# Three layers, one core: the put-aside tiles of the second layer are loaded three f ahead, and the sums of W_in's quarters are stored once and loaded afterwards

## The chip, the core and the metric

One NeuronCore of a Trainium2 chip runs the whole program. Its engines are TensorE (PE, with weight loads as PEld), VectorE (DVE), ScalarE (ACT), GpSimd (POOL) and SyncE (SP), which issues nearly all DMAs. The metric is the device time of one execution in microseconds; lower is better.

## What is computed

```python
x = _attn(q, k, v, phi)             # 8 batches x 576 tokens, read as 4608 x 512
g, val = xn @ w_gate, xn @ w_val    # first layer, xn = rms-normed x, d_ff 1536
x = (silu(g) * val) @ w_out
h = x @ w_in                        # second layer, 512 -> 2048
r = np.maximum(h, 0.0)
return ((r * r) @ w_out).astype(np.float32)
```

All is float32. Each operand of a matmul is split into a high and a low part (`split`, L64: ScalarE makes the high part, VectorE the low one), and three matmuls make one product. This case is about the second layer.

## The kernel before

The 4608 tokens are 9 blocks of 512 (`T`). `phase_b` (L999) takes them in four wide pairs (p = 0 to 3, two blocks each) and a last pair of half the width (p = 4, one block in two halves). In the profile the five pairs start at about 871, 1049, 1233, 1417 and 1598 us.

The first product, x @ W_in, is done for a pair by a Strassen-like scheme of seven products. W_in's 16 tiles of 128 columns (f) are taken two at a time: eight quarters q = 0 to 7, with f0 = 2q and f1 = 2q + 1. A quarter's weights are four pieces A11, A12, A21, A22 and four sums S1 to S4 of them. The order of the products in a quarter is b1 (A11), b2 (A12), b6 (S2), b7 (S3), b5 (S1), b3 (S4), b4 (A22); they rotate through four PSUM banks. VectorE adds them up to c11, c21, c22, c12, applies relu and square, and the results of the first block of the pair go on as `gh`/`gl`.

While quarter q is multiplied, the weights of q + 1 are made ready: `wi2_sums` (L909, four GpSimd operations write `si_s`), `wi2_split` "a" (A11, A12: `wiha`, `wila`), "b" (the four sums, 128 x 1024: `wihb`, `wilb`), "c" (A22: `wihc`, `wilc`). At the end of the quarter `wi2_load` (L902) loads the raw weights of q + 2 in two DMAs of 256 KB (`si`), the second of which waits until `wilc` has been made from its buffer. All this is done anew in each of the five pairs.

The second product, with W_out, goes in pieces between the products: `z` for the first block of the pair, f by f. What belongs to the second block is put aside in DRAM: c12 and c22 are stored as `gd[f]` (256 KB each). After the eight quarters the kernel finishes `z`, stores the block (`out_store`, four tiles of 256 KB; each store writes its 128 rows as chunks of 32 rows, so its pattern in DRAM begins with a dimension of 4, or is two stores with a dimension of 2 where a batch ends), and then runs the loop over f = 0 to 16 (L1114) for the second block, `zz`: load `gd[f]` into `gb` (two buffers, one load ahead), split it, and multiply f - 1, 12 matmuls. In the same loop `x2_step` makes the next pair's x operands, from `xr`, which `x2_load` loads in two halves: the first at the end of quarter 6, the second at f = 6 of the loop. The output stores of the second block come in quarters 0 and 1 of the next pair.

Each engine takes its instructions in the order of the program, and SP too: a DMA that has to wait holds up those behind it.

Of the kernel before, what the change touches and what calls it, by code (L numbers as in the profile page):

```python
# [9 lines left out]
F32 = mybir.dt.float32  # L10
# [10 lines left out]
P = 128  # L21
# [31 lines left out]
class Kernel:  # L53
# [67 lines left out]
    def run(self):  # L121
        nc, tc, ctx = self.nc, self.tc, self.ctx
        self.raws, self.started, self.wo_next, self.st = {}, [], [], {}
        const = ctx.enter_context(self.pool("const"))
        dram = ctx.enter_context(self.pool("dram", space=DRAM))
        ps = ctx.enter_context(self.pool("ps", space=PSUM))
        self.ps, self.dram = ps, dram

        self.ident = const.tile([P, P], F32, name="ident")
        make_identity(nc, self.ident)  # L130
        self.ones = const.tile([P, P], F32, name="ones")
        nc.vector.memset(self.ones, 1.0)
        self.g_sb = const.tile([P, KC], F32, name="g_sb")
        self.idle = self.ones.bitcast(BF16)

        self.y1 = [dram.tile([P, KC, HALF], F32, name=f"y1_{n}") for n in range(2 * B)]
        self.w1d = [dram.tile([P, KC * DM], F32, name=f"w1_{n}") for n in range(NCH)]
        self.w2d = {(c, f): dram.tile([P, DM], F32, name=f"w2_{c}{f}") for f in range(NF2) for c in "iz"}

        wa, up = self.pool("wa"), self.pool("up")  # L140
        self.wa, self.up = wa.__enter__(), up.__enter__()
        cms = []
        with tc.using_default_side("right"):
            for name in ("raw", "wst", "at"):
                cms.append(self.pool(name))
                setattr(self, name, cms[-1].__enter__())

        with tc.manual_schedule():
            self.make_plan()
            self.prologue()  # L150
            self.phase_a(0, NI * (B - 1) + 3)


        for cm in reversed(cms):
            cm.__exit__(None, None, None)
        with tc.using_default_side("right"):
            self.wb = ctx.enter_context(tc.tile_pool(name="wb1", bufs=1, reuse_waits="tile"))
        self.w2, self.w2_raw, self.w2_loaded, self.wi, self.x2 = {}, {}, 0, {}, {}
        with tc.manual_schedule():
            self.phase_a(NI * (B - 1) + 3, NI * B + 1)  # L160
        up.__exit__(None, None, None)
        wa.__exit__(None, None, None)
        self.wb2 = ctx.enter_context(tc.tile_pool(name="wb2", bufs=1, reuse_waits="tile"))
        with tc.manual_schedule():
            self.phase_b()
# [663 lines left out]
    def phase_a(self, start, end):  # L829
        nc = self.nc  # L830
        if not start:
            self.us = {}
        for n in range(start, end):
            first = True
            if n < len(self.items):
                b, hf, f, first, _ = self.items[n]
                gp = self.ps.tile([P, T], F32, tag="g", name=f"g{n}")[:, 0:HALF]
                self.mm_in(gp, b, hf, f, 0)
                self.slot(n, "a")
                sl = self.up.tile([P, HALF], F32, tag="sl", bufs=2, name=f"sl{n}")  # L840
                nc.scalar.activation(sl, gp, AF.Silu)  # L841
                vp = self.ps.tile([P, T], F32, tag="v", name=f"v{n}")[:, 0:HALF]
                self.mm_in(vp, b, hf, f, 1)
                self.slot(n, "b")
                nc.vector.tensor_tensor(sl, sl, vp, op=ALU.mult)  # L845
                uh = self.up.tile([P, HALF], F32R, tag="uh", bufs=3, name=f"uh{n}")
                ul = self.up.tile([P, HALF], F32R, tag="ul", bufs=3, name=f"ul{n}")
                self.split(uh, ul, sl, lo_engine="pool")
                self.us[n] = (uh, ul)
                self.slot(n, "c")  # L850

            second = 0 < n and n - 1 < len(self.items) and self.items[n - 1][3]
            for m in () if second else (n - 2, n - 1) if first else (n - 2,):
                if m >= 0:
                    self.mm_out(m)
            self.slot(n, "d")
            if NF1 <= n < NI and n % 6 == 3:
                t = self.up.tile([P, KC, HALF], F32, tag="st", name=f"yl{n}")
                nc.sync.dma_start(t, self.y1[2 * b + hf])
                self.st["y"] = t  # L860
            i = n - NI * (B - 1)
            if i == 4:
                self.x2_load(0, 0)
                self.wi2_load(0)
            elif i == 13:
                self.x2_load(0, 1)
            if 6 <= i < 13:
                self.x2_step(0, 0, i - 6)
            elif 15 <= i < 22:
                self.x2_step(0, 1, i - 15)  # L870
            elif i == 5:
                self.wi2_sums(0)
            elif i in (13, 14, 22):
                self.wi2_split(0, "abc"[(13, 14, 22).index(i)])
            elif i == 23:
                self.wi2_load(1)
                self.wo2_next(0)


# [19 lines left out]
        self.split(hi, lo, self.w2_raw.pop(i))  # L899
        self.w2[i] = (hi, lo)  # L900

    def wi2_load(self, q):  # L902
        self.wi_raw = []
        for i in range(2):
            t = self.wb.tile([P, DM], F32, tag=f"si{i}", name=f"si{q}_{i}")
            self.nc.sync.dma_start(t, self.w2d["i", 2 * q + i])
            self.wi_raw.append(t)

    def wi2_sums(self, q):  # L909
        eng = self.nc.gpsimd  # L910
        s0, s1 = self.wi_raw
        s = self.wb.tile([P, 4, 2 * P], F32, tag="ss", name=f"si{q}_s")
        a11, a12, a21, a22 = s0[:, 0 : 2 * P], s0[:, 2 * P : DM], s1[:, 0 : 2 * P], s1[:, 2 * P : DM]
        eng.tensor_tensor(s[:, 0], a21, a22, op=ALU.add)  # L914
        eng.tensor_tensor(s[:, 1], s[:, 0], a11, op=ALU.subtract)
        eng.tensor_tensor(s[:, 2], a11, a21, op=ALU.subtract)
        eng.tensor_tensor(s[:, 3], a12, s[:, 1], op=ALU.subtract)
        self.wi_sum = s

    def wi2_split(self, q, part):  # L920
        pool = self.wb2 if q % 2 else self.wb
        src = {
            "a": self.wi_raw[0],
            "c": self.wi_raw[1][:, 2 * P : DM],
            "b": self.wi_sum.rearrange("p s n -> p (s n)"),
        }[part]
        n = src.shape[-1]
        hi = pool.tile([P, n], F32R, tag=f"wih{part}", name=f"wih{part}{q}")
        lo = pool.tile([P, n], F32R, tag=f"wil{part}", name=f"wil{part}{q}")
        self.split(hi, lo, src)  # L930
        for i, k in enumerate({"a": ("A11", "A12"), "c": ("A22",), "b": ("S1", "S2", "S3", "S4")}[part]):
            self.wi[k, q % 2] = tuple(t[:, 2 * P * i : 2 * P * (i + 1)] for t in (hi, lo))

    def width(self, p):
        return T if p < NB // 2 else T // 2
# [63 lines left out]
    def phase_b(self):  # L999
# [22 lines left out]
        def z_pieces(n, y, key, f):  # L1022
# [6 lines left out]

            return [partial(do, 0), partial(do, 2)]  # L1030

        for _ in range(2):
            self.wo2_next(NF2)
        for p in range(NPAIR):
# [3 lines left out]
            for q in range(NQ):  # L1038
                if q == 1:
                    y = [self.ps.tile([P, T], F32, tag=f"y{c}", name=f"z{p}_{c}") for c in range(KC)]  # L1040
                nq = (q + 1) % NQ if p < NPAIR - 1 or q < NQ - 1 else None
                if q:
                    for f in (2 * q - 2, 2 * q - 1):
                        self.pieces += z_pieces(2 * p, y, (p, f), f)
                f0, f1 = 2 * q, 2 * q + 1
                more = nq is not None
                b1 = product("A11", "X11")
                p1 = work("cp", 3, f"p1_{p}_{q}", w)
                nc.scalar.activation(p1, b1, AF.Copy)
# [1 line left out]
                c11 = work("c", 4, f"c11_{p}_{q}", w)  # L1051
                nc.vector.tensor_tensor(c11, b2, p1, op=ALU.add)
                if more:
                    self.wi2_sums(nq)
                piece()
                b6 = product("S2", "T2")
                u = work("cp", 3, f"u_{p}_{q}", w)
# [4 lines left out]
                c21 = work("c", 4, f"c21_{p}_{q}", w)  # L1062
                nc.vector.tensor_tensor(c21, b7, u, op=ALU.add)
                if more:
                    self.wi2_split(nq, "a")
                piece()
                b5 = product("S1", "T1")
                nc.vector.tensor_tensor(u, b5, u, op=ALU.add)
# [5 lines left out]
                else:  # L1074
                    self.g_split(p, f1, 1, c22)
                if more:
                    self.wi2_split(nq, "b")
                piece()
                b3 = product("S4", "X22")
                c12 = work("c", 4, f"c12_{p}_{q}", w)  # L1080
# [8 lines left out]
                sq(c21)  # L1089
                self.g_split(p, f1, 0, c21)  # L1090
                if more:
                    self.wi2_split(nq, "c")
                    if p < NPAIR - 1 or q < NQ - 2:
                        self.wi2_load((q + 2) % NQ)
                piece()
                for _ in range(2):
                    self.wo2_next(NF2)
                if q == NQ - 2 and p + 1 < NPAIR:
                    self.x2_load(p + 1, 0)
            f0, f1 = NF2 - 2, NF2 - 1  # L1100
            for c in range(KC):
                self.mm_z(y, self.gs[p, f0], f0, c)
# [7 lines left out]
                self.out_store(2 * p, y, c, c + 1)  # L1110

            y = [self.ps.tile([P, T], F32, tag=f"y{c}", name=f"zz{p}_{c}") for c in range(KC)]
            loaded = {}
            for f in range(NF2 + 1):  # L1114
                while len(loaded) < min(f + 2, NF2):
                    i = len(loaded)
                    loaded[i] = work("gb", 2, f"gb{p}_{i}", w)
                    nc.sync.dma_start(loaded[i], gd[i])
                if f < NF2:
                    self.gs.pop((p, f), None)  # L1120
                    key = ("b", p, f)
# [79 lines left out]
```

## Time and profile before

| | |
|---|---|
| Times | 1716.00, 1712.21, 1714.54 us; median 1714.54 |
| The profiled execution | 1711.83 us, its span 1709.9 us |
| TensorE busy | 1565.5 us, 92% of the span |
| VectorE, ScalarE, GpSimd busy | 1061.7, 623.6, 508.7 us |
| Mean granted TensorE clock | 0.955 |
| DMA | 227.98 MB, 133 GB/s over the span |

All times within the span are from its start. The share of busy time is an average over stages; the second layer takes the time from about 840 us on. A matmul's duration in the trace overlaps the next one's: the pace is the difference of two starts. The granted clock is given as a share of the full 2.4 GHz, so 0.50 is 1.2 GHz. "DMA share" is the mean busy share of the 16 DMA engines.

### The profile page before, as it was taken

What the parts mean: (1) busy time and instruction counts of PE and PEld (TensorE: products, weight loads), DVE (VectorE), ACT (ScalarE), POOL (GpSimd) and SP (SyncE); (2) the same over time, 40 slices, a digit from 0 to 9 for tenths busy, and PEclk for the clock granted to TensorE, in tenths of its full rate; (3) what the DMA queues carried; (4) which work ended last, traced back from release to release, by engine and by line L of the source; (5) the groups of instructions that cost most, each with busy time, mean ns of one, the idle gap of its engine ahead of it and who ended that gap; (6) DMA issues with size and microseconds to landing.
All of it is one profiled execution on the core that took longest, in us unless ns stands there. A gap on an engine that the chain in (4) does not pass through costs nothing.

```text
span 1709.9 us, 26676 instructions
## 1 busy us (share of the span) xinstructions
PE 1565.5 (92%) x10302; PEld 1319.1 (77%) x10302; DVE 1061.7 (62%) x1744; ACT 623.6 (36%) x1240; POOL 508.7 (30%) x547
## 2 busy tenths in 40 slices
PE   5487999999999999999999969996999889996987
PEld 4266798888889798889988857885788668885876
DVE  4887756657574755535568845674577546773575
ACT  1566535354444435343433323222322232222232
POOL 1476544344443534234222200221012200220021
PEclk7688999999999999999999989998999989998999
DMA  9797573755546562322123333223322332223211
GB/s 258 226 278 278 214 219 135 219 184 168 176 170 185 193 194 110 113 93 97 46 88 110 118 102 89 87 70 121 99 85 70 116 112 81 74 74 117 73 46 43
DMA packets 129455, 227.98 MB, mean 133 GB/s; under 512 B 27440, under 2 KB 69424, under 8 KB 123184
## 3 DMA queue, kind: packets, MB, share of 16 engines
q1 hardware_dynamic: 125744, 223.39, 41.3%
q10 hardware_dynamic: 3584, 2.88, 0.7%
q8 instruction: 81, 1.33, 0.3%
q14 instruction: 46, 0.38, 0.1%
HBM read 174.72 MB, written 51.51 MB: 132 GB/s over the span
## 4 chain that ended last, share of the span: by engine, by line
PE 74%; DVE 8%; DMA 8%; ACT 4%; POOL 3%; issue 2%; SPq 2%; ACTq 0%; DVEq 0%; POOLq 0%
PE y L811 5%; PE y L812 5%; PE y L813 5%; PE h_S L985 4%; PE z L1141 3%; PE z L1143 3%; PE h_S L987 3%; PE z L1142 3%; PE h_S L986 3%; PE zz L1141 3%; DMA gb<-gd 3%; PE zz L1142 3%; PE zz L1143 3%; PE v L795 3%; PE g L795 3%; PE h_A L985 3%
## 5 line engine op out<-in xcount | busy, mean ns | idle before, releaser
L71 POOL TENSOR_TENSOR ul<-sl,uh 128x288 fp32r<-128x288 f32 x192 | 166.5, 867 | 363.7 <-ACT uh L67 363.3
L811 PE MATMUL y<-uh,woh 128*128 128x288 f32 x768 | 235.4, 307 | 0.0
L914 POOL TENSOR_TENSOR si_s<-si 128x256 f32<-128x256 f32 x40 | 33.5, 837 | 677.8 <-DMA si<-w_i 563.2
L812 PE MATMUL y<-uh,wol 128*128 128x288 f32 x768 | 227.7, 297 | 0.8 <-POOL wol L71 0.8
L813 PE MATMUL y<-ul,woh 128*128 128x288 f32 x768 | 226.5, 295 | 0.0
L845 DVE TENSOR_TENSOR sl<-sl,v 128x288 f32<-128x288 f32 x192 | 86.0, 448 | 178.6 <-PE v L797 140.0
L67 ACT ACTIVATE gh<-c 128x512 fp32r<-128x512 f32 (+1 forms) x96 | 53.8, 561 | 350.4 <-DVE c L1020 341.9
L1141 PE MATMUL zz<-bzh,gbh 128*128 128x512 f32 x256 | 104.6, 409 | 60.0 <-ACT gbh L67 60.0
L811 PEld LDWEIGHTS y<-uh,woh 128*128 128x128 f32 x768 | 144.7, 188 | 16.4 <-issue 15.5
L67 ACT ACTIVATE uh<-sl 128x288 fp32r<-128x288 f32 x192 | 85.2, 444 | 182.9 <-DVE sl L845 182.9
L812 PEld LDWEIGHTS y<-uh,wol 128*128 128x128 f32 x768 | 145.2, 189 | 1.7 <-POOL wol L71 1.0
L813 PEld LDWEIGHTS y<-ul,woh 128*128 128x128 f32 x768 | 145.0, 189 | 0.0
L841 ACT ACTIVATE sl<-g 128x288 f32<-128x288 f32 x192 | 78.4, 408 | 165.2 <-PE g L797 159.6
L795 PE MATMUL g<-anh,wph 128*128 128x288 f32 x384 | 119.9, 312 | 14.9 <-ACT sl L841 10.1
L1141 PE MATMUL z<-bzh,gh 128*128 128x512 f32 x320 | 127.0, 397 | 0.1
L1143 PE MATMUL z<-bzh,gl 128*128 128x512 f32 x320 | 126.0, 394 | 0.0
L1142 PE MATMUL z<-bzl,gh 128*128 128x512 f32 x320 | 125.6, 392 | 0.0
L795 PE MATMUL v<-anh,wph 128*128 128x288 f32 x384 | 120.4, 313 | 5.1 <-DVE sl L845 5.1
L796 PE MATMUL g<-anl,wph 128*128 128x288 f32 x384 | 115.4, 301 | 0.0
L796 PE MATMUL v<-anl,wph 128*128 128x288 f32 x384 | 115.3, 300 | 0.0
L797 PE MATMUL v<-anh,wpl 128*128 128x288 f32 x384 | 114.9, 299 | 0.0
L797 PE MATMUL g<-anh,wpl 128*128 128x288 f32 x384 | 114.2, 297 | 0.0
(214 smaller groups left out, 3966.8 us busy)
## 6 DMA issues: line engine op xcount, KB each, us to landing
w<-w SPq DMA_DIRECT2D x48, 1024.0 KB
si<-w_i SPq DMA_DIRECT2D x80, 256.0 KB
q<-in_q_dram SPq DMA_DIRECT2D x128, 144.0 KB
gd<-c SPq DMA_DIRECT2D x64, 256.0 KB
gb<-gd SPq DMA_DIRECT2D x64, 256.0 KB
y<-ys SPq DMA_DIRECT2D x16, 576.0 KB
raw_i<-in_moe_w_in_dram SPq DMA_DIRECT2D x16, 512.0 KB
raw_z<-in_moe_w_out_dram SPq DMA_DIRECT2D x16, 512.0 KB
```

The costliest lines, as they stand in the source:

```text
L67: nc.scalar.activation(hi, src, AF.Copy)
L71: eng.tensor_tensor(lo, src, hi.bitcast(F32), op=ALU.subtract)
L795: nc.tensor.matmul(out, wh[:, r, cs], ah[:, r], start=(r == 0), stop=False)
L796: nc.tensor.matmul(out, wh[:, r, cs], al[:, r], start=False, stop=False)
L797: nc.tensor.matmul(out, wl[:, r, cs], ah[:, r], start=False, stop=(r == NR - 1))
L811: nc.tensor.matmul(y, hi[:, cs], uh, start=first, stop=False)
L812: nc.tensor.matmul(y, lo[:, cs], uh, start=False, stop=False)
L813: nc.tensor.matmul(y, hi[:, cs], ul, start=False, stop=last)
L985: nc.tensor.matmul(out, wh[:, cs], xh, start=(kk == 0), stop=False)
L1141: nc.tensor.matmul(y[c], gh[:, cs], oh, start=(f == 0), stop=False)
L1142: nc.tensor.matmul(y[c], gh[:, cs], ol, start=False, stop=False)
L1143: nc.tensor.matmul(y[c], gl[:, cs], oh, start=False, stop=(f == NF2 - 1))
```

## The change

- `gb` has four buffers instead of two. At the end of quarter 6, behind `x2_load`, the first three `gd` tiles are loaded (`gb_load(3)`); in the loop over f, tile f + 3 is loaded at step f.
- The sums are made in the first pair only. There, `wi2_split` "b" also stores the split sums `wihb`, `wilb` into 16 DRAM tiles `sd` (512 KB each, two per quarter). From the second pair on, `wi2_sums` and `wi2_split` "b" do nothing, and `wi2_load` first loads the two `sd` tiles of the quarter into the same buffers, then `si` as before. The pair's number p is handed through.

```diff
+        self.sd = [[dram.tile([P, 4 * 2 * P], F32, name=f"sd{q}{i}") for i in "hl"] for q in range(NF2 // 2)]
...
-    def wi2_load(self, q):
+    def wi2_load(self, p, q):
         self.wi_raw = []
+        if p:
+
+            t = self.wi2_tiles(q, "b", 4 * 2 * P)
+            for x, d in zip(t, self.sd[q]):
+                self.nc.sync.dma_start(x.bitcast(F32), d)
+            self.wi2_set(q, "b", t)
         for i in range(2):
             t = self.wb.tile([P, DM], F32, tag=f"si{i}", name=f"si{q}_{i}")
             self.nc.sync.dma_start(t, self.w2d["i", 2 * q + i])
             self.wi_raw.append(t)
 
-    def wi2_sums(self, q):
+    def wi2_sums(self, p, q):
+        if p:
+            return
...
+    def wi2_split(self, p, q, part):
+        if p and part == "b":
+            return
...
+        t = self.wi2_tiles(q, part, src.shape[-1])
+        self.split(*t, src)
+        self.wi2_set(q, part, t)
+        if part == "b":
+            for x, d in zip(t, self.sd[q]):
+                self.nc.sync.dma_start(d, x.bitcast(F32))
...
+        def gb_load(end):
+            while len(loaded) < min(end, NF2):
+                i = len(loaded)
+                loaded[i] = work("gb", 4, f"gb{p}_{i}", w)
+                nc.sync.dma_start(loaded[i], gd[i])
...
                 if more:
-                    self.wi2_split(nq, "c")
+                    self.wi2_split(np, nq, "c")
                     if p < NPAIR - 1 or q < NQ - 2:
-                        self.wi2_load((q + 2) % NQ)
+                        self.wi2_load(p + (q + 2) // NQ, (q + 2) % NQ)
                 piece()
                 for _ in range(2):
                     self.wo2_next(NF2)
-                if q == NQ - 2 and p + 1 < NPAIR:
+                if q == NQ - 2 and wide:
                     self.x2_load(p + 1, 0)
+                    loaded = {}
+                    gb_load(3)
...
-            loaded = {}
             for f in range(NF2 + 1):
-                while len(loaded) < min(f + 2, NF2):
-                    i = len(loaded)
-                    loaded[i] = work("gb", 2, f"gb{p}_{i}", w)
-                    nc.sync.dma_start(loaded[i], gd[i])
+                gb_load(f + 4)
```

## Rows read from the trace of the kernel before

**Rows 1.** The page: engine, busy us (share of span) x instructions.

```profile
PE 1565.5 (92%) x10302; PEld 1319.1 (77%) x10302; DVE 1061.7 (62%) x1744; ACT 623.6 (36%) x1240; POOL 508.7 (30%) x547
```

**Rows 2.** Busy time by stretch: engines (x instructions), then clock, DMA share, GB/s.

```profile
1115.00:1145.00 30.00, 30.00 (x132) 24.50 (x131) 22.75 (x33) 7.28 (x12) 7.32 (x8) 1.00 0.22 71
1674.00:1682.00 8.00, 5.79 (x26) 4.71 (x25) 6.19 (x14) 2.55 (x7) 0.02 (x1) 0.79 0.21 66
```

**Rows 3.** Waits, us in total, times, longest: whole span; then 1595 to 1710 us.

```profile
PE zz L1141 <- ACT gbh L67: 60.0, 7, 14.3
...
PE h_S L985 <- DVE c L1081: 4.9, 4, 2.3
PE h_S L985 <- DVE c L1088: 2.4, 5, 0.7
```

**Rows 4.** Timeline of TensorE: start, us, operation [idle before <- releaser].

```profile
992.30 0.39 PE L1143 MATMUL z<-bzh,gl 128*128 128x512 f32 x1
1006.90 0.79 PE L1141 MATMUL zz<-bzh,gbh 128*128 128x512 f32 x1 [14.21 <-ACT gbh L67]
...
1012.12 0.40 PE L1141 MATMUL zz<-bzh,gbh 128*128 128x512 f32 x1
...
1558.42 0.80 PE L1141 MATMUL zz<-bzh,gbh 128*128 128x512 f32 x1 [14.21 <-ACT gbh L67]
```

**Rows 5.** Timeline of SP's queue around the first wide pair's end.

```profile
974.78 3.80 SPq L947 DMA_DIRECT2D xr<-y  x6
...
987.26 3.03 SPq L906 DMA_DIRECT2D si<-w_i  x2
991.31 3.23 SPq L1170 DMA_DIRECT2D out_dram<-os  x4
994.64 24.66 SPq L1118 DMA_DIRECT2D gb<-gd  x8
```

**Rows 6.** The chain that ended last, 950 to 1250 us: start, us, what.

```profile
994.64 11.50 DMA gb<-gd
```

**Rows 7.** Busy time by stretch, columns as in rows 2, during the stall.

```profile
994.00:996.00 2.00, 0.00 (x0) 0.00 (x0) 0.00 (x0) 0.00 (x0) 1.59 (x3) 0.74 0.22 70
...
998.00:1000.00 2.00, 0.00 (x0) 0.00 (x0) 0.00 (x0) 0.00 (x0) 0.00 (x0) 0.50 0.79 296
...
1002.00:1004.00 2.00, 0.00 (x0) 0.00 (x0) 0.00 (x0) 0.00 (x0) 0.00 (x0) 0.50 0.26 102
```

**Rows 8.** Busy time by stretch: weight loads of the first layer; x loads.

```profile
302.00:303.00 1.00, 1.00 (x10) 1.00 (x9) 1.00 (x4) 0.68 (x2) 0.15 (x1) 1.00 1.01 426
...
1026.00:1032.00 6.00, 5.34 (x24) 4.10 (x22) 0.69 (x1) 0.75 (x2) 0.00 (x0) 1.00 0.83 238
```

**Rows 9.** Timelines of ScalarE, VectorE, TensorE: quarter 1 of pairs two and three.

```profile
1076.55 0.63 ACT L67 ACTIVATE wiha<-si 128x512 fp32r<-128x512 f32 x1 [4.34 <-DMA si<-w_i]
1078.54 0.69 DVE L1070 TENSOR_TENSOR c<-h_S,u 128x512 f32<-128x512 f32 x1
1079.68 0.39 PE L985 MATMUL h_A<-X11h,wiha 128*128 128x512 f32 x1
...
1259.36 0.63 ACT L67 ACTIVATE wiha<-si 128x512 fp32r<-128x512 f32 x1 [2.94 <-DMA si<-w_i]
1263.89 0.39 PE L985 MATMUL h_A<-X11h,wiha 128*128 128x512 f32 x1
```

**Rows 10.** The chain that ended last, in the last pair.

```profile
1641.49 2.76 DMA si<-w_i
...
1647.83 1.07 ACT wihb L67
...
1648.92 1.23 DVE wilb L71
1650.15 0.34 DVE c L1081
...
1662.24 0.34 DVE c L1081
```

More of the change, by code (lines that the diff above doesn't have):

```diff
@@ L863, in phase_a @@
                 self.x2_load(0, 0)
-                self.wi2_load(0)
+                self.wi2_load(0, 0)
             elif i == 13:
@@ L871, in phase_a @@
             elif i == 5:
-                self.wi2_sums(0)
+                self.wi2_sums(0, 0)
             elif i in (13, 14, 22):
-                self.wi2_split(0, "abc"[(13, 14, 22).index(i)])
+                self.wi2_split(0, 0, "abc"[(13, 14, 22).index(i)])
             elif i == 23:
-                self.wi2_load(1)
+                self.wi2_load(0, 1)
                 self.wo2_next(0)
@@ L918, in wi2_sums, with wi2_tiles, wi2_set @@
         self.wi_sum = s
-    def wi2_split(self, q, part):
+    def wi2_tiles(self, q, part, n):
         pool = self.wb2 if q % 2 else self.wb
+        return [pool.tile([P, n], F32R, tag=f"wi{i}{part}", name=f"wi{i}{part}{q}") for i in "hl"]
+    def wi2_set(self, q, part, t):
+        for i, k in enumerate({"a": ("A11", "A12"), "c": ("A22",), "b": ("S1", "S2", "S3", "S4")}[part]):
+            self.wi[k, q % 2] = tuple(x[:, 2 * P * i : 2 * P * (i + 1)] for x in t)
+    def wi2_split(self, p, q, part):
+        if p and part == "b":
+            return
         src = {
@@ L926, in wi2_split @@
         }[part]
[L927 to L932, printed above, removed]
+        t = self.wi2_tiles(q, part, src.shape[-1])
[4 more added lines that the diff above has]
+                self.nc.sync.dma_start(d, x.bitcast(F32))
     def width(self, p):
@@ L1040, in phase_b @@
                     y = [self.ps.tile([P, T], F32, tag=f"y{c}", name=f"z{p}_{c}") for c in range(KC)]
-                nq = (q + 1) % NQ if p < NPAIR - 1 or q < NQ - 1 else None
+                np, nq = p + (q + 1) // NQ, (q + 1) % NQ
                 if q:
@@ L1045, in phase_b @@
                 f0, f1 = 2 * q, 2 * q + 1
-                more = nq is not None
+                more = np < NPAIR
                 b1 = product("A11", "X11")
@@ L1053, in phase_b @@
                 if more:
-                    self.wi2_sums(nq)
+                    self.wi2_sums(np, nq)
                 piece()
@@ L1064, in phase_b @@
                 if more:
-                    self.wi2_split(nq, "a")
+                    self.wi2_split(np, nq, "a")
                 piece()
@@ L1076, in phase_b @@
                 if more:
-                    self.wi2_split(nq, "b")
+                    self.wi2_split(np, nq, "b")
                 piece()
```

## The prediction

> **What bounds the kernel now.** I read the page's busy times first, then the table of waits, then the timelines of single engines where a wait ends last. TensorE is busy for 92% of the span [rows 1], and in the second layer's main loop it is busy for all of a 30 us stretch at the full granted clock [rows 2]. A cheaper VectorE, ScalarE or GpSimd step there gains nothing; only stretches where TensorE stands still count. The table of waits names them [rows 3]: 60.0 us in 7 waits for the split of a put-aside tile (`gb`), and 4.9 and 2.4 us in the half-width last pair.
>
> The 60 us are four long stalls at the start of the second block of each wide pair and three short ones in its middle. The first long one lasts 14.21 us, and the fourth is the same [rows 4]. What ends it is a chain of four 256 KB output stores issued from 991.31 on, then the first `gb` load, issued at 994.64 [rows 5], 11.50 us until that load lands at 1006.14 [rows 6], and 0.76 us for the split until TensorE starts at 1006.90. While it is awaited the DMA engines are busy for 0.26 of their time at 102 GB/s; only between 998 and 1000 did they reach 0.79 [rows 7]. I read this so: the stores use a quarter of the engines, about 25 GB/s each, and the `gb` load, spread over all 16, is done on the other twelve at once but waits on these four behind 1 MB of stores: 1 MB at 102 GB/s is 10.3 us. The Trainium skill, DMA: Bandwidth & Descriptors, section Why a DMA increments its semaphore by 16 and not by 1, says that a transfer runs on the largest number of engines up to 16 that divides the slowest dimension of both its patterns; the store's pattern in DRAM begins with a dimension of 4. Its section Queues, rings and completion order adds that each engine consumes its ring in order. The trace agrees with both (0.26 and 102 GB/s). By the second, the fourth tile can't pass the stores, and the loads ahead give the 28.0 us worked out below; without it they would give the 61.5 us of rival 1.
>
> **The loads ahead.** Now three tiles are loaded in the loop's seventh quarter, long before the stores. The fourth is still issued behind the last out_store, as the first is today; a fourth buffer doesn't change its place in the queue. So f = 0 to 2 can run during the drain, and f = 3 waits where f = 0 waits now.
>
> Worked out: f = 0 is split after the last ScalarE copy and starts some 1 us after 992.7. Three f at full clock take 3 x 2.73 = 8.2 us (12 matmuls each, at 30.00 us for 132 of them [rows 2]), until about 1002. The fourth tile lands at 1006.1 plus a delay d, and f = 3 starts at 1006.9 + d. Today f = 0 starts there. The gain is three f, 8.2 us, less d.
>
> d comes from the 1 MB of sums that the change puts on the queue just ahead of the stores, at about 987, before the `si` pair [rows 5]. Spread over 16 engines it is 64 KB on each. Nearest prices: 1 MB weight loads in the first layer move at 426 GB/s (2.4 us), the x and `gb` loads of the second layer at 238 GB/s (4.2 us) [rows 8]. The sums have 4 KB rows, nearer the former. As the engines are partly idle around 988 to 992, not all of it is seen: d is 0 to 2.8 us, and I take 1.2. Gain 7.0 us per pair (5.4 to 8.2), 4 pairs: **28.0 us**.
>
> The clock: after 14 us of idling the granted clock is 0.50, and f = 0 takes 5.22 us (1006.90 to 1012.12) instead of 2.73 [rows 4, 7]. It fell some 2.3 us after the engine stopped (the mean of 0.74 over 994 to 996). The remaining idle is about 6 us, so I expect the same fall and no gain; if the clock stayed up, 2.4 us more per pair, 9.6 in all.
>
> The three short stalls, 60.0 - 4 x 14.2 = 3.1 us, come because a `gb` load is queued behind the next pair's x loads. With three tiles ahead it has 8 us more, so they go, with about 0.3 us each of slowed first matmuls: **4.0 us**. What would be late next is ScalarE, which waits there for the x load before its next split; its slack is about 2 us.
>
> **The sums.** From the second pair on, each quarter drops four GpSimd operations, a 128 x 1024 ScalarE copy (1.07 us) and a VectorE subtraction (1.23) [rows 10], and adds two 512 KB loads on SP's queue, which wait for the matmuls of the same quarter, but the store queued before them waits for these anyway. In wide pairs this is beside a full TensorE: zero. In the first pair each quarter adds two stores, 1 MB. SP waits for the split's two halves, and the next store behind waits for later VectorE work anyway; 71 GB/s are in use in the main loop [rows 2], and 1 MB per 15 us adds 68. Nobody awaits their landing, so I take zero; work added gains nothing, and at worst one `si` load comes late behind them, once, by the 4.2 us that 1 MB takes at the slower pace of [rows 8].
>
> In the last pair the sums are on the path. The chain goes through the `si` load (2.76 us), GpSimd's four operations (1644.25 to 1647.83, 3.6 us), the copy, the subtraction and then the rest of the quarter, and comes round after 12.1 us (1650.15 to 1662.24 [rows 10]). TensorE alone needs less: 24 matmuls at 0.227 us and 42 of half the columns at half of that, an estimate from [rows 2], are 10.2 us. Without the sums the `si` load needs only to land before the next `a` split, and TensorE sets the pace. The waits for L1081 and L1088 are 7.3 us together [rows 3]. The first, 2.26 us, stays: there `si` lands late behind the stores, and the 1 MB ahead of it costs as much as the missing sums give back. So 5.1 us go, and with them the slow clock around 1678 (0.79 over 8 us, 1.7 us [rows 2]), of which I count 1.5: **6.6 us** (0 to 9).
>
> **A new wait.** In the second quarter of a pair the `si` load is already late, behind output stores: ScalarE waits for it until 1076.55 in the second pair, the sum c22 starts at 1078.54 (0.69 us), and the product that needs its bank starts at 1079.68 without idling [rows 9]. The sums' 1 MB now stands ahead of `si`, on the busy four engines too: 2.4 us more. TensorE then idles about 2.3 us in the second pair, less the 0.4 that goes, and up to 2.4 us of slow clock follow (I take 1.2). In the third pair `si` is awaited until 1259.36 and the product starts at 1263.89; c22 ends 2.7 us after the wait by the same steps, at 1262.0, so there is 1.9 us of slack and 0.5 is seen. In the fourth there is slack enough. **3.5 us lost** (0 to 8).
>
> **Sum**: 28.0 + 4.0 + 6.6 - 3.5 = 35.1 us. The profiled execution took 1711.83 us, so 1676.7; the median of the runs shown is 1714.54, which gives 1679.4. I say 1679. With the bounds of d, clock, last pair and the new wait the gain is 20 to 50 us, 1665 to 1695.
>
> **Rivals.**
> 1. *The stall goes whole.* If `gb` loads pass the stores, or the stores drain faster once no loads stand among them, f = 3 finds its tile. Then all but some 1 us of each 14.2 goes, and the slow clock behind it: 4 x 13.2 + 3 x 2.4 + 1.5 = 61.5 instead of 28.0, time about 1646. Against: the drain at 102 GB/s goes on with nothing else moving [rows 7]. Chance 0.10.
> 2. *The sums crowd the queue.* If 1 MB of sums takes 4.2 us, as at 238 GB/s, with d at 2.8 or more and `si` late in each pair, the loads ahead still give 4 x 5 + 4, the last pair 3, and the new wait costs 10: 17 us, about 1697. Chance 0.10.
> 3. *Slower.* The same place, but the sums land at the pace of the output stores. Each us of d costs 4 us over the pairs, and each us by which `si` lands later costs some 4 more at the second quarters, all beyond the first 2.4 us. The 35 us are spent when the 1 MB takes about 2.4 + 35 / 8 = 6.8 us, under 155 GB/s. At 102 GB/s it is 10.3 us: 63 us lost, 28 net, about 1742. For it: `si`, `gd`, x and sums all go through one queue. Against: the tiles span 128 partitions as `gb` does, which ran at 296 GB/s beside the stores. Chance 0.05.
> 4. *It does less than it says*: the early loads are issued late, because SP stands at the x loads of 974.78 [rows 5], or f = 0 waits for something else. Then only the middle stalls and the last pair gain, 7 us, about 1707. Against: in the trace these x loads are issued in 3.80 us, and 9 us of free queue follow. Chance 0.05.
>
> **How the numbers follow.** The forecast has 0.70. Its own range is 1665 to 1695; the range for 8 in 10 takes in rival 2 and part of rival 1's side: 1658 to 1699. A change of 0.2% (3.4 us) is about what a measurement of this kernel can tell from none. Faster: forecast, rivals 1 and 2, and most of rival 4: 0.92. Same: 0.03. Slower: 0.05.
>
> **What would show it.** In the changed profile: `zz` starts within 2 us of the last `z`; a TensorE gap of about 6 us waits for the fourth `gb` split, three f later, with the clock at 0.50 behind it; the short gaps are gone; GpSimd is idle after the first pair; in the last pair TensorE's waits after the third quarter vanish and a quarter takes 10 to 10.5 us; a gap of about 2 us stands at the third quarter of the second pair. A gap under 2 us at the fourth `gb`, or one over 8, would show that the reading of the queue is wrong.

## The result, and the profile after

The changed kernel takes 1671.05 us (1669.37 to 1675.26, four runs) against 1715.27 us before (1712.21 to 1716.36, four runs): a ratio of 0.9749, interval 0.9726 to 0.9771, 44.2 us less. The prediction said 1679, with 1658 to 1699 as its range.

The profiled execution of the changed kernel took 1675.26 us, its span 1673.5 us. Some 8.5 us of that lie in the first layer: the second layer's first product starts at 879.5 us there, at 871.0 before and at 872 to 876 in all the experiments. TensorE is 8.5 us late there at 645 us already, ahead of the first instruction that the change touches. So I compare the second layer alone, from that product to TensorE's start of the last output product of the last pair: 1701.94 - 871.0 = 830.9 us before, 1664.70 - 879.5 = 785.2 after, **45.7 us less**. Lines have moved: the loop's product `zz` is now L1163 to L1165 (L1141 before), the x @ W_in products are L1003 to L1005 (L985), and the sum `u` of the third result is L1092 (L1068).

TensorE on the page, as in [rows 1]: engine, busy us (share of span) x instructions.

```profile
PE 1570.8 (94%) x10302; PEld 1318.2 (79%) x10302; DVE 1012.5 (61%) x1712; ACT 590.2 (35%) x1208; POOL 397.6 (24%) x419
```

GpSimd has lost 128 operations and 111 us, ScalarE and VectorE 32 each (33 and 49 us). Most of that work lay beside a busy TensorE; where the time came from is read from what TensorE waits for. The table of waits of the changed kernel's second layer: us in total, times, longest.

```profile
PE zz L1163 <- ACT gbh L67: 22.5, 9, 5.0
PE h_A L1003 <- DVE u L1092: 2.6, 2, 2.2
```

The 60.0 us for the `gb` split [rows 3] are 22.5 now, and in the last pair the waits of 4.9 and 2.4 for the sums are gone, and one of 2.2 for `u` stands there. TensorE's timeline of the changed kernel (start, us, operation, idle before and releaser) has all that is left, but for repeats in other pairs:

```profile
1001.71 0.50 PE L1163 MATMUL zz<-bzh,gbh 128*128 128x512 f32 x1 [0.53 <-ACT gbh L67]
1015.43 0.79 PE L1163 MATMUL zz<-bzh,gbh 128*128 128x512 f32 x1 [4.86 <-ACT gbh L67]
1031.48 0.50 PE L1163 MATMUL zz<-bzh,gbh 128*128 128x512 f32 x1 [0.83 <-ACT gbh L67]
...
1253.72 0.47 PE L1003 MATMUL h_A<-X11h,wiha 128*128 128x512 f32 x1 [0.43 <-DVE u L1092]
...
1539.05 0.79 PE L1163 MATMUL zz<-bzh,gbh 128*128 128x512 f32 x1 [4.94 <-ACT gbh L67]
...
1594.80 0.36 PE L1003 MATMUL h_A<-X11h,wiha 128*128 128x256 f32 x1 [2.22 <-DVE u L1092]
```

Where one gap of 14.21 us stood at f = 0 [rows 4], there is 0.53 at f = 0 and a gap of 4.86 three f later; the other pairs have 4.98, 4.83 and 4.94. Why that gap is there is read from SP's queue and the chain of the changed kernel (start, us, what):

```profile
989.07 1.70 SPq L1054 DMA_DIRECT2D gb<-gd  x3
...
994.86 0.38 SPq L909 DMA_DIRECT2D wihb<-sd1h  x1
995.34 0.40 SPq L909 DMA_DIRECT2D wilb<-sd1l  x1
995.83 2.12 SPq L913 DMA_DIRECT2D si<-w_i  x2
999.81 3.25 SPq L1192 DMA_DIRECT2D out_dram<-os  x4
1003.11 18.52 SPq L1054 DMA_DIRECT2D gb<-gd  x7
```

```profile
1003.11 11.53 DMA gb<-gd
```

The three early loads go out 10 us before the stores, the fourth behind them, and it lands 11.53 us after its issue, as the first did before (11.50 [rows 6]). The sums and `si` lie between. Busy time by stretch (TensorE, its weight loads, VectorE, ScalarE, GpSimd, then granted clock, DMA share, GB/s), the changed kernel:

```profile
996.00:998.00 2.00, 2.00 (x10) 1.65 (x9) 1.03 (x2) 0.84 (x2) 0.00 (x0) 1.00 0.99 263
998.00:1000.00 2.00, 2.00 (x11) 1.65 (x10) 0.14 (x1) 0.60 (x1) 0.00 (x0) 1.00 0.96 383
...
1012.00:1014.00 2.00, 0.00 (x0) 0.00 (x0) 0.00 (x0) 0.00 (x0) 0.00 (x0) 1.00 0.27 99
...
1190.00:1194.00 4.00, 4.00 (x10) 3.08 (x11) 3.15 (x5) 1.27 (x3) 0.00 (x0) 0.50 0.21 73
...
1606.00:1650.00 44.00, 44.00 (x278) 39.70 (x277) 30.48 (x77) 12.06 (x31) 0.00 (x0) 1.00 0.41 143
```

From 996 to 1000 the sums and `si`, issued from 994.86 on, fill the DMA engines, and at 999.81 the first store goes out. The rest of these loads is through 1 us later: the share is 0.74 at 283 GB/s from 1000 to 1001 and 0.27 at 27 GB/s from 1001 to 1002. Before, with no sums, the first store met the rest of `si` in the same way (0.93 from 991 to 992). In the gap (1012 to 1014) the share is 0.27 at 99 GB/s, the same drain as in [rows 7]. Behind the gap of the second pair the clock is at 0.50 (1.2 GHz) for four us. And in the last pair TensorE is busy for all of 44 us.

The table has the length of the parts in us, from the start of the first product of one to that of the next, in TensorE's timelines. "Loops" is the eighth quarter with the loop behind it, in the four wide pairs.

| | before | after | gain |
|---|---|---|---|
| loops | 77.44, 77.33, 77.34, 74.73 | 67.94, 67.95, 67.92, 67.50 | 35.5 |
| last pair, quarters 0 to 2 | 10.52, 12.28, 14.94 | 10.53, 12.89, 12.13 | 2.2 |
| last pair, quarters 3 to 6 | 11.05, 12.45, 12.06, 14.81 | 10.50, 10.52, 10.50, 10.53 | 8.3 |
| second pair, quarters 1 and 2 | 15.23, 15.76 | 15.34, 15.25 | 0.4 |
| third pair, quarters 1 and 2 | 15.22, 15.15 | 15.82, 15.24 | -0.7 |
| first pair, quarters 1 to 6 | 15.14 to 15.29 | 15.14 to 15.30 | 0 |

These add up to 45.7.

### The profile page after: what moved, and what is told of

It reads as the page before. It is cut to its first block, busy times and chain, and to the rows that moved or that the text cites. A ratio compares the mean times of both kernels' runs of the same rounds, so it can differ in the third digit from the quotient of the medians.

```text
span 1673.5 us, 26576 instructions
## 1 busy us (share of the span) xinstructions
PE 1570.8 (94%) x10302; PEld 1318.2 (79%) x10302; DVE 1012.5 (61%) x1712; ACT 590.2 (35%) x1208; POOL 397.6 (24%) x419
## 4 chain that ended last, share of the span: by engine, by line
PE 77%; DMA 7%; DVE 7%; ACT 4%; issue 2%; POOL 2%; SPq 1%; ACTq 0%; DVEq 0%; POOLq 0%
PE y L812 5%; PE y L813 5%; PE y L814 5%; PE z L1163 4%; PE z L1165 4%; PE z L1164 4%; PE h_S L1005 4%; PE h_S L1003 4%; PE h_S L1004 4%; PE v L796 3%; PE h_A L1003 3%; PE h_A L1005 3%; PE h_A L1004 3%; PE wp L523 3%; DMA gb<-gd 3%; PE g L796 3%
## 5 line engine op out<-in xcount | busy, mean ns | idle before, releaser
L1163 PE MATMUL z<-bzh,gh 128*128 128x512 f32 x320 | 126.3, 395 | 0.0
L1163 PE MATMUL zz<-bzh,gbh 128*128 128x512 f32 x256 | 104.7, 409 | 22.5 <-ACT gbh L67 22.5
L1165 PE MATMUL z<-bzh,gl 128*128 128x512 f32 x320 | 125.9, 393 | 0.0
L541 DVE TENSOR_TENSOR wpl<-wp,wph 128x512 fp32r<-128x512 f32 x96 | 61.3, 679 | 80.2 <-ACT wph L535 80.2
```

The source lines that it names most:

```text
L1163: nc.tensor.matmul(y[c], gh[:, cs], oh, start=(f == 0), stop=False)
L1165: nc.tensor.matmul(y[c], gl[:, cs], oh, start=False, stop=(f == NF2 - 1))
```

## The experiments

The theory was the prediction's: stores that use four of the 16 DMA engines hold up the fourth tile, so a pair gains three f and keeps a gap; the sums are worth something in the last pair alone. Against it stand the rivals: that the sums on the same queue set when the fourth tile and `si` land, or that the gap has another cause than the stores' drain.

### Each half alone

The changed kernel without the sums: they are made anew in every pair.

```diff
-        self.sd = [[dram.tile(...)]]
-        if p:        # in wi2_load: the loads of sd
-            ...
-        if p:        # in wi2_sums
-            return
-        if p and part == "b":        # in wi2_split
-            return
-        if part == "b":        # the stores of sd
-            ...
```

> The changed kernel with the loads ahead kept and the sums made anew in each pair, as before. Theory (the fourth tile waits for the output stores on their few engines, whatever else is queued): the gap before the fourth tile stays 4.8 to 5.0 us in each wide pair, the loops gain 9 us in pairs one to three and 7 in the fourth, 35 us together, about 1680; the last pair takes 88 us from its first product to that of its last quarter, as before. Rival (the 1 MB of sums ahead of the stores makes the fourth tile late): the gap is 2 to 4 us, and the gain of the loads alone is 40 us or more, about 1673.

It took 1679.76 us, 0.9797 (0.978 to 0.9814), 33.1 us less than before. TensorE's timeline of this kernel:

```profile
1009.64 0.79 PE L1149 MATMUL zz<-bzh,gbh 128*128 128x512 f32 x1 [4.62 <-ACT gbh L67]
```

The other gaps are 4.59, 4.99 and 4.46, three of the four just under the 4.8 to 5.0 expected, and none near the 2 to 4 of the rival. The loops take 68.19, 67.89, 68.19 and 67.61 us: 35.0 less than before. The last pair is no shorter (89.2 us to its last quarter, 88.1 before), and the second quarters are as before. So the loops' gain is that of the loads ahead, and it is the same with no sums on the queue.

The kernel before with the sums, and two `gb` buffers as it had:

```diff
-                loaded[i] = work("gb", 4, f"gb{p}_{i}", w)
+                loaded[i] = work("gb", 2, f"gb{p}_{i}", w)
...
-                    loaded = {}
-                    gb_load(3)
...
+            loaded = {}
-                gb_load(f + 4)
+                gb_load(f + 2)
```

> The kernel before with the sums stored and loaded, and two buffers and one load ahead for the put-aside tiles, as before. Theory (the sums' loads are through before the stores start, so they delay nothing there): the long gaps stay at 14.2 us, the last pair gains 10.5 us, the second quarters lose under 1 us: about 1705. Rival (the sums delay the stores by some us): gaps of 15.4 to 17 us, the last pair's gain is eaten up, 1710 or more.

It took 1704.39 us, 0.9951 (0.9933 to 0.9969), 8.4 us less than before. TensorE's timeline:

```profile
1009.49 0.80 PE L1162 MATMUL zz<-bzh,gbh 128*128 128x512 f32 x1 [14.10 <-ACT gbh L67]
...
1624.56 0.36 PE L1003 MATMUL h_A<-X11h,wiha 128*128 128x256 f32 x1 [2.25 <-DVE u L1092]
```

The gap of 14 us stays, and the last pair's quarters are 10.53, 12.92, 12.15, then 10.50 to 10.53, as in the changed kernel. Quarter 1 of the second and third pair grew by 0.8 and 0.4 us. The two halves give 33.1 + 8.4 = 41.5 us; each interval is some 3 us to either side, so this agrees with the 44.2 of both together.

### More tiles ahead

If the gap is just the drain less the tiles at hand, a fourth early tile takes one f (2.73 us) from it, and six early tiles fill it.

```diff
-                    gb_load(3)
+                    gb_load(4)
```

> The changed kernel with four instead of three tiles loaded ahead of the stores, in the same four buffers; the fifth is issued behind the stores. Theory: one more f of 2.73 us is covered, the gap falls from 4.9 to 2.1 to 2.3 us and stands before the fifth tile; a pause as short as that leaves the granted clock at full speed, so 2.4 us of slow matmuls go too: 5 us per wide pair, 20 together, about 1650. Rival (the clock falls after a 2 us pause too): 11 us, about 1660.

It took 1659.73 us, 0.9678 (0.9663 to 0.9692). The gaps are 2.28, 2.23, 2.32 and 2.27: 4.9 less 2.7, as the theory has it. TensorE's timeline and the busy time by stretch behind each of the four gaps:

```profile
1010.83 0.80 PE L1163 MATMUL zz<-bzh,gbh 128*128 128x512 f32 x1 [2.28 <-ACT gbh L67]
...
1356.49 0.50 PE L1163 MATMUL zz<-bzh,gbh 128*128 128x512 f32 x1 [2.32 <-ACT gbh L67]
```

```profile
1010.00:1014.00 4.00, 3.17 (x8) 2.46 (x9) 2.49 (x4) 1.78 (x3) 0.00 (x0) 0.58 0.33 95
...
1183.00:1187.00 4.00, 2.76 (x7) 1.94 (x8) 2.08 (x4) 1.78 (x3) 0.00 (x0) 0.71 0.33 100
...
1356.00:1360.00 4.00, 3.51 (x14) 2.63 (x15) 2.83 (x5) 1.59 (x3) 0.00 (x0) 1.00 0.29 82
...
1528.00:1532.00 4.00, 3.61 (x9) 2.57 (x10) 2.57 (x6) 1.81 (x5) 0.00 (x0) 0.68 0.26 81
```

The clock fell behind three of the four gaps and stayed at 1.00 behind the longest. That part of the expectation, a clock that stays up, missed, and the time came out where the rival had put it, though the gaps themselves are the theory's. Quarter 1 of the second pair grew too, from 15.34 in the changed kernel to 16.87 us, as `si` comes 1.5 us later there, counted from the start of the pair.

```diff
-                loaded[i] = work("gb", 4, f"gb{p}_{i}", w)
+                loaded[i] = work("gb", 6, f"gb{p}_{i}", w)
-                    gb_load(3)
+                    gb_load(6)
-                gb_load(f + 4)
+                gb_load(f + 6)
```

> The changed kernel with six buffers and six tiles loaded ahead of the stores instead of three; the seventh tile is issued behind the stores. Theory (each further tile covers 2.73 us of the same drain): six tiles cover 16.4 us, the drain takes some 14 us, so the gap before the seventh tile is under 1 us, the slow clock behind it goes too, and each wide pair gains 4.9 + 2.4 us more: 29 us, about 1642. Rival (the wait is for something that moves with the load, not a fixed drain): a gap of some us stays, now before the seventh tile, and the gain is under 10 us.

It took 1641.86 us, 0.9583 (0.9569 to 0.9597). TensorE's timeline:

```profile
996.88 0.50 PE L1163 MATMUL zz<-bzh,gbh 128*128 128x512 f32 x1 [0.53 <-ACT gbh L67]
1019.75 0.50 PE L1163 MATMUL zz<-bzh,gbh 128*128 128x512 f32 x1 [0.40 <-ACT gbh L67]
...
1068.37 0.47 PE L1003 MATMUL h_A<-X11h,wiha 128*128 128x512 f32 x1 [1.25 <-DVE u L1092]
```

The gap is gone, with the slow clock behind it, and the loops take 60.0 to 61.1 us. At the end of quarter 1 the second pair now waits for 1.25 us and the third for 0.51, where the changed kernel has none and 0.43.

### Stores on more engines

The other way to shorten the drain is to change the stores. Each output store is split into four of 32 rows, so that its pattern in DRAM begins with a dimension of 32 in place of 4.

```diff
-            c = c0
-            while c < c0 + P:
-                b, k = divmod(c, S)
-                e = min(c0 + P, (b + 1) * S)
-                nc.sync.dma_start(rows[b, k // M : k // M + (e - c) // M], o[c - c0 : e - c0])
-                c = e
+            for i in range(P // M):
+                b, k = divmod(c0 + i * M, S)
+                nc.sync.dma_start(rows[b, k // M], o[i * M : (i + 1) * M])
```

> The changed kernel with each output store of the second layer issued as four stores of 32 rows, so that the pattern in DRAM begins with 32 instead of 4; the same bytes. Theory (the stores drain slowly because they use a quarter of the engines): in the stall the share of the DMA engines rises well above 0.26, the fourth tile lands within 3 us of its issue; the sixteen issues take SP 6 to 9 us, so it is issued at about the time when it is needed, and the gap falls from 4.9 to 0 to 3 us: 1645 to 1660. Rival (the bound is the write to DRAM itself, at about 100 GB/s): the fourth tile lands 11 to 15 us after the first store as now, the gap stays 5 us or grows with the longer issue: 1670 or more.

On top of the change it took 1650.74 us, 0.9631 (0.9617 to 0.9646), 20.3 us less than the change alone. SP's queue, the chain, the busy time by stretch and TensorE's timeline:

```profile
993.47 7.39 SPq L1190 DMA_DIRECT2D out_dram<-os  x16
1000.91 9.78 SPq L1054 DMA_DIRECT2D gb<-gd  x7
```

```profile
1000.91 2.79 DMA gb<-gd
```

```profile
994.00:1000.00 6.00, 5.35 (x22) 3.79 (x21) 4.52 (x8) 3.72 (x7) 0.00 (x0) 1.00 0.56 145
...
1018.00:1026.00 8.00, 5.93 (x25) 4.26 (x24) 4.99 (x8) 4.60 (x8) 0.00 (x0) 1.00 0.82 247
```

```profile
1020.64 0.50 PE L1163 MATMUL zz<-bzh,gbh 128*128 128x512 f32 x1 [2.00 <-ACT gbh L67]
```

The DMA share during the stores is 0.56 where it was 0.26, and the fourth tile lands 2.79 us after its issue, not 11.5. The Trainium skill, DMA: Bandwidth & Descriptors, section Why a DMA increments its semaphore by 16 and not by 1, gives a slowest dimension of 32 all 16 engines and one of 4 only four; 0.26 agrees with four of 16, and 0.56 with more than four. What it costs is SP's time: 16 issues in 7.39 us, where four took 3.25. The fourth tile's gaps are 0.24, 0.22, 0.73 and 1.83 us. In the middle of the loop there are pauses of 2.00, 1.43 and 1.89 us, longer than in the changed kernel. ScalarE splits the tile there right behind x, for which it has waited 4.72, 4.15 and 4.61 us, so its wait for x is what is late next. Quarter 1 has no stalls in any wide pair, where `si` no longer stands behind a slow drain, and the last pair's quarters are 10.50 to 10.67.

The same edit on the kernel before, without the change:

> The kernel before with each output store of the second layer issued as four stores of 32 rows; nothing else of the change. Theory: the drain goes, and the first tile waits only for the sixteen issues on SP and its own landing: 7.4 us after the first store plus 2.8 us plus 0.8 us for the split, that is a gap of 9 to 10 us instead of 14.2; the raw weights in the second quarters come in time, which the last pair shows in its third quarter: 20 to 25 us gained, about 1690. Rival (the write itself is the bound): the gap stays at 14 us.

1692.54 us, 0.9872 (0.9857 to 0.9886). TensorE's timeline and the chain:

```profile
1003.48 0.79 PE L1141 MATMUL zz<-bzh,gbh 128*128 128x512 f32 x1 [9.62 <-ACT gbh L67]
```

```profile
999.96 2.75 DMA gb<-gd
```

The load lands in 2.75 us, and still 9.62 us pass, as it is issued only behind 7.4 us of store issues. So the stores' issue and their drain each hold the tile up. The split is worth 22 us alone and 20 with the change; the change is worth 44 alone and 42 with the split.

### The place of the sums in the queue

The prediction charged the sums with a delay of the fourth tile and of `si`. Here `si` is loaded first, the sums behind it.

```diff
     def wi2_load(self, p, q):
         self.wi_raw = []
+        for i in range(2):
+            ...        # the two loads of si
         if p:
             ...        # the two loads of sd
-        for i in range(2):
-            ...        # the two loads of si
```

> The changed kernel with the raw weights loaded ahead of the sums on the queue, instead of behind them. Theory (what stands ahead of the raw weights in the quarters with output stores delays them and, through the a split, TensorE): in the last pair the second and third quarter take 27.2 - 2.3 = 23 to 24 us together instead of 25.0, the 0.43 us stall in the third pair goes: 1 to 2.5 us, about 1669. Rival (the raw weights wait only for the stores, and the sums ahead of them cost nothing): no difference, 1671. Against both: the sums now wait behind the second raw load, which waits for the c split; if they came late for their products, the wide pairs' quarters would grow beyond 15.2 us.

It took 1673.54 us, 0.9757 (0.9743 to 0.9772): no gain over the change. TensorE's timeline, SP's queue and a row of busy time by stretch:

```profile
1011.97 0.79 PE L1162 MATMUL zz<-bzh,gbh 128*128 128x512 f32 x1 [5.92 <-ACT gbh L67]
...
1602.89 0.36 PE L1002 MATMUL h_A<-X11h,wiha 128*128 128x256 f32 x1 [0.93 <-DVE c L1093]
```

```profile
990.34 3.08 SPq L907 DMA_DIRECT2D si<-w_i  x2
993.51 0.38 SPq L912 DMA_DIRECT2D wihb<-sd1h  x1
993.99 0.38 SPq L912 DMA_DIRECT2D wilb<-sd1l  x1
995.29 4.03 SPq L1191 DMA_DIRECT2D out_dram<-os  x4
```

```profile
996.00:998.00 2.00, 1.40 (x5) 0.50 (x4) 1.33 (x4) 1.98 (x4) 0.00 (x0) 1.00 0.93 342
```

The quarters gained more than expected: the third pair's stall is gone, and in the last pair quarters 1 and 2 take 10.50 + 11.63 = 22.13 us in place of 25.02. But the gaps at the fourth tile grew to 5.92, 6.61, 5.99 and 5.57 us, by 0.6 to 1.6 each, and the loops to 69.0, 69.29, 69.12 and 68.21, 4.3 us in all. The second `si` load waits for `wilc`, and the sums behind it go out at 993.51, only 1.8 us ahead of the stores; in the changed kernel they go out 4.95 us ahead (994.86 to 999.81). From 996 to 998, with the first store issued, the DMA engines still work at 342 GB/s on what stands ahead of it. With that, SP needs 3.10 to 4.03 us for the four stores, against 3.17 to 3.25 in the changed kernel, and the fourth tile lands 11.70 to 13.43 us after its issue, against 11.53 to 11.70. So the delay that the prediction called d is real, but only where the sums come late. The expected time was missed, because this wasn't counted.

### Both remedies

Six tiles ahead and the split stores together:

> Six tiles ahead and stores of 32 rows together. Theory: the loops of the wide pairs are already without gaps with six tiles ahead (60 us), and stay so; the stores of 32 rows remove what is left behind the output stores of the second blocks, 1.4 and 0.7 us in the second quarters and 4.0 us in the last pair: about 1636. Rival (the sixteen issues on SP make the x operands or the tiles late): 1642 or more.

1634.06 us (1632.27 to 1634.49), 0.9525 (0.9509 to 0.9541): the fastest, 37 us below the change. The busy time of nearly the whole second layer, and TensorE's timeline:

```profile
876.00:1624.00 748.00, 745.41 (x3404) 614.85 (x3403) 485.85 (x806) 199.87 (x374) 21.95 (x24) 1.00 0.46 153
```

```profile
997.54 0.50 PE L1163 MATMUL zz<-bzh,gbh 128*128 128x512 f32 x1 [0.53 <-ACT gbh L67]
...
1496.29 0.50 PE L1163 MATMUL zz<-bzh,gbh 128*128 128x512 f32 x1 [0.53 <-ACT gbh L67]
```

The loops take 59.97 to 60.01 us, the last pair's quarters 10.49 to 10.59, and TensorE is idle for 2.6 of 748 us at full clock. The waits treated here were nearly all that it lost in this layer.

## Why the prediction was right, and where its terms were off

The direction and the mechanism held; the gain was 44 to 46 us where 35.1 was forecast.

| term | predicted | measured |
|---|---|---|
| three f of each wide pair, less d | 28.0 | 32.4 |
| clock behind the gap | 0 | 0.2 |
| short stalls in the middle | 4.0 | 2.9 |
| last pair | 6.6 | 10.5 |
| the new wait | -3.5 | -0.3 |
| first pair's stores of sums | 0 | 0 |
| sum | 35.1 | 45.7 |

The first three measured terms are worked out from the distances between the starts of `zz` matmuls, against 0.227 us each; together they give 35.5, as the loops' lengths do. Two slips in the prediction's own figures move nothing: 1 MB at 238 GB/s takes 4.4 us, not 4.2, and the terms of its new wait add up to 3.6, not 3.5.

**The loads ahead.** The fourth tile waits where the first did: it lands 11.53 us after issue, and f = 3 starts 14.63 us after the last `z`, where f = 0 started 14.60 after it [rows 4]; in the other pairs it is 14.61 to 14.75, where it was 14.59 to 14.64. So rival 1, that the stall goes whole, fell. The term of d was mis-sized: 1.2 us taken, 0.07 measured in the mean of the four pairs. The 1 MB of sums goes out 4.95 us ahead of the first store, and that is enough, as the DMA share above shows; in the kernel with `si` first it goes out 1.8 us ahead, and the delay is there. The lower bound, zero, was nearly right, for a reason that the prediction itself named: the DMA engines were partly idle there (before, a share of 0.34 in the mean from 986 to 991). The forecast named a gap of about 6 us; it is 4.9.

**The clock.** Expected to fall still, and it did, in all four pairs. It fell some 3.0 to 4.3 us after TensorE had stopped (in the first pair a mean of 0.92 from 1014 to 1015), where the prediction read 2.3 from one gap before. Over a gap's first matmuls, the excess above 0.227 us each adds up to 9.3 us before and 9.0 after. A gap a third as long costs as much behind it.

**The short stalls.** The prediction let all three go. Two did; the first pair's stayed at 0.83 us (1031.48). The prediction had said that ScalarE's wait for x would be late next, and the trace shows it: ScalarE waits 4.60 us for x and splits the tile of 1031.48 right behind it, at 1030.81. The slack that the prediction gave it, 2 us, was not there in that pair. ScalarE's timeline:

```profile
1030.27 0.63 ACT L67 ACTIVATE X11h<-xr 128x512 fp32r<-128x512 f32 x1 [4.60 <-DMA xr<-y]
1030.81 0.61 ACT L67 ACTIVATE gbh<-gb 128x512 fp32r<-128x512 f32 x1
```

**The last pair.** Its quarters 3 to 6 came to 10.50 to 10.53 us, as forecast (10 to 10.5), and TensorE was idle there for 5.0 us before, as counted (5.1). But the quarters gained 8.3, not 6.6: TensorE's busy time for the same work fell as well, from 45.46 to 42.05 us. Of these 3.4 us the forecast had counted 1.5, from one dip of the clock [rows 2]. The clock is at 1.00 in the rest of these quarters but for 0.95 from 1674 to 1678, so most of what it hadn't counted isn't the clock; what it is stays open. For quarters 1 and 2 the forecast let the 2.26 us stall stay and nothing go. In place of that, the stall for the sums (L1081, 2.26 us) went whole, and the lateness of `si` shows at the end of quarter 1: a wait of 1.23 us for `u`, which [rows 3] don't list, became 2.22. Idle time fell from 3.65 (with 0.16 for L1088) to 2.22, and the clock's dip behind it got smaller, from 0.57 over 1626 to 1630 to 0.69 over 1596 to 1600; the three quarters are 2.2 us shorter together. The wait before, in TensorE's timeline:

```profile
1620.91 0.36 PE L985 MATMUL h_A<-X11h,wiha 128*128 128x256 f32 x1 [1.23 <-DVE u L1068]
```

**The new wait.** Here a step failed in its reading. The prediction let the product wait for c22. In the changed kernel TensorE waits for `u`, the operation before it. Timelines of ScalarE, VectorE and TensorE, quarter 1 of the second pair and of the third:

```profile
1076.68 0.63 ACT L67 ACTIVATE wiha<-si 128x512 fp32r<-128x512 f32 x1 [5.48 <-DMA si<-w_i]
...
1077.96 0.69 DVE L1092 TENSOR_TENSOR u<-h_S,u 128x512 f32<-128x512 f32 x1
...
1078.79 0.47 PE L1003 MATMUL h_A<-X11h,wiha 128*128 128x512 f32 x1
...
1251.61 0.63 ACT L67 ACTIVATE wiha<-si 128x512 fp32r<-128x512 f32 x1 [5.96 <-DMA si<-w_i]
...
1252.89 0.68 DVE L1092 TENSOR_TENSOR u<-h_S,u 128x512 f32<-128x512 f32 x1
```

The product starts 2.11 us after ScalarE's split both times (1076.68 to 1078.79, 1251.61 to 1253.72). Before, it started 3.13 and 4.53 us after it [rows 9], so there was slack of 1.0 and 2.4 us, not none and 1.9. And `si` came later by 1.1 us in the second pair and 3.0 in the third (counted from the start of the pair, 27.26 to 28.40 and 25.86 to 28.88), where 2.4 was taken for both. Less the slack that is 0.1 and 0.6 us, and quarter 1 grew by 0.11 and 0.60. The gap of about 2 us that the prediction expected in the second pair is not there. The six-tile kernel fits too: there `si` comes 1.3 us later still, and quarter 1 takes 16.63 in place of 15.34.

**The rivals.** 2 and 3 needed d of 2.8 us or more, or loads of the sums as slow as the stores; the stretch that holds them ran at 263 to 383 GB/s. 4 needed late early loads; they went out at 989.07, 12 us before f = 0. The 45.7 us lie within the bounds that the prediction gave for its gain, 20 to 50, and near their top, because three of the unknown costs came out at or beyond the favourable end of their ranges: d near zero, the new wait at 0.3, the last pair at 10.5 (above its 9).

## What to carry to other kernels

Where a load waits behind stores on one queue, look at the DMA share during the wait: 0.26 says that four engines work, and then changing the stores' shape (20 to 22 us here) and loading earlier (33 us) are both open; beyond the change six tiles gave 29 us, the split 20, both 37. How many tiles to load ahead follows from the drain over the time of one tile: 14.6 us over 2.73 is more than five, and three left 4.9 us, four 2.3, six none. Before a wait is charged to a late operand, look for the instruction that frees the buffer: one operation earlier in the chain was 0.5 to 1 us of slack here.

## What the runs showed of the hardware

The length of a pause between 1.8 and 2.3 us didn't decide whether the clock fell. With four tiles ahead it fell behind pauses of 2.28, 2.23 and 2.27 us and stayed at 1.00 (2.4 GHz) behind 2.32 and, in the middle of the third loop, 2.15; with the split stores on the change it fell behind 1.89 and 1.83 us and stayed behind 2.00 and 1.43. In the last pair the wait at the end of quarter 1 is nearly the same in four kernels: behind 2.22 (the change), 2.25 (the sums alone) and 2.23 us (six tiles) the clock was at 0.50 for a time, and behind 2.25 (four tiles) it stayed at 1.00. Each gap of 4.8 us or more in the changed kernel brought it to 0.50 (1.2 GHz). With four tiles ahead the matmuls behind a pause lost 1.6 to 2.0 us where the clock fell, against their 0.227 us each, and 0.4 where it stayed, so a gap of some 2 us has two prices, and the prediction of one holds to no better than that. What decided between the two, these runs do not show.
